# Two-stage kernel on one core: all attention row chunks scaled by VectorE, a new hand-written order with a new bank plan, pooled SBUF rings, and unordered half-row writes

## The chip, the cores and the metric

The kernel runs on one core of one Trainium2 chip. Time is device time in microseconds (us) for one execution; the figures of a kernel are the median of its runs. A profile is one execution taken by the hardware profiler. In this text PE is TensorE (PEld its weight loads), DVE is VectorE, ACT is ScalarE, POOL is GpSimd and SP is the queue that issues most DMAs.

## What is computed

Two blocks follow each other. The first is an attention between a sequence and a small state, both ways, for 8 batches, 8 heads, 512 positions, 32 state rows and 64 columns:

```python
scores = scale * x @ state.T            # softmax over the 32 state rows
xread = softmax(scores) @ state         # 512 rows per head
scores2 = scale * state @ x.T           # softmax over the 512 positions
sread = softmax(scores2) @ x            # 32 rows per head
attn = concatenate([xread, sread])      # (8, 8, 544, 64)
```

The heads are then laid side by side, giving 544 rows of 512 per batch. The second block scores each row with a gate vector and sends the 128 best rows of each batch through two dense layers; all rows are written, the chosen ones changed:

```python
scores = einsum('bsd,d->bs', x, w_gate)
top = argpartition(-scores[b], 128)[:128]
ye = maximum(x[b, top] @ w1, 0) @ w2    # 512 -> 1024 -> 512
out[b, top] = x[b, top] + sigmoid(scores[b, top])[:, None] * ye
```

All arithmetic that decides the result is 32 bit.

## The kernel before

The program is a list of named pieces (function `add`), each with an engine, a function that issues its instructions, the pieces it comes after, and the buffers it takes or uses. Nothing is scheduled automatically: the string `ORDER` lists every piece by hand, and `carry_out` issues them in that order, so each engine works through its own pieces strictly in the listed order. A number behind `@` in the list names the PSUM bank that the piece takes (the tile `banks` has 8 of them, 512 float32 each per partition; `scores` takes two in a row, `read` four). An entry `~n@k` is n transposes of the identity into bank k, whose result nobody reads. Waits between engines follow from the data, and from memory: a tile or a bank that is taken again waits for its last readers.

For each batch b the pieces are:

- `ldx`: loads of x (1 MB in two or four cuts), `ldy`: a second load of x in another layout for batches 6 and 7.
- `turn`/`turned`: transposes of x on PE (L408) and their copies out of PSUM on ACT (L417); batches 6 and 7 use block transposes on DVE instead (`blocks`, L397).
- `stturn`/`stkept`: the transposed state for two batches at a time.
- `scores`: both score matrices at once (L433), in two banks. From them DVE takes the column maximum and subtracts it (`xmax`, `xspread`, `xsub`), ACT takes the exponential (`xexp`); for batches 0 and 1 this is done in halves. `smax` (DVE, L480), `sexp` (ACT, L484) and `ssum` do the same for the other softmax.
- `read`: the attention rows with their sum and gate score as two extra columns (L546; for odd batches, listed in `READ64`, L523, which reads 64 rows at a time from a tile `st_2` that POOL fills with the pieces `beside`). There are two halves r = 0, 1 per batch, each in banks 0 to 3. `zsum` (L562, L563) forms the reciprocal sums, `gate` (L569 to L574) the gate scores, and `rows b.c` scales chunk c of 128 positions and 512 columns into `xs`. Chunks 0 and 2 are scaled by DVE (L556; for odd batches two instructions at L534), chunks 1 and 3 by ACT in eight activations of 64 columns (L554, L532): `ACT_ROWS` lists these.
- `turna`/`turneda`, or for batches 4 to 7 `ablocks`/`aout`/`ain` by DVE and a round trip through DRAM: the transposed weights of the other softmax; `sread` (L627) and `srows` produce the state rows. `stx` and `sts` store both.
- `sgate`, `heads`, `sscore`, `row`/`rowk`/`srowk` or `rowblk`/`rowout`/`rowin`, `win`, `over`, `off`, `oh`, `pick`, `index`, `picked`: the choice of the 128 rows by comparing all scores with each other. `fetch` gathers the rows from DRAM with an indirect DMA on POOL (L659); `parts` on POOL splits the scores for it.
- `xg`/`xgk`: the transposes of the chosen rows (L818, L821); `first b.f`: eight pieces of the first layer (L840); `relu` (L843); `second`: the second layer (L862) in four pieces of two steps each; `add` (L865) adds the gated result to the rows; `put` writes them back with an indirect DMA. The last batch does the second layer in two column halves with two `put`s, so that the first can go early.

Buffers: x has five tiles, the transposed x nine. The exponentials (`eT`, 2), the other softmax (`a`, 2), its block transpose (`a_b`, 1) and its transpose (`aT`, 2) have rings of their own, all with the same number of bytes per tile. The transposed state of all batches has one fixed tile, `st_T`.

## Time and profile before

| what | value |
|---|---|
| median of 3 runs | 212.33 us (211.43 to 213.33) |
| the profiled execution, time of the run | 210.6 us |
| the profiled execution, span from its first to its last instruction | 208.8 us |
| mean granted clock of TensorE in it | 0.961 |

The page gives busy time by engine, the span in 40 slices, DMA queues, the chain of work that ended last, and the costliest groups of instructions (line, engine, operation, tiles, shapes, count, then busy us and mean ns of one, then the engine's idle time ahead of them and what ended it). Other views of the same trace are busy time in chosen windows, the timeline with the idle time before each instruction and its releaser, and the chain in order of time. The lines on which the argument rests stand in the prediction.

### The profile page before, as it was taken

What the parts mean: (1) busy time and instruction counts of PE and PEld (TensorE: products, weight loads), DVE (VectorE), ACT (ScalarE), POOL (GpSimd) and SP (SyncE); (2) the same over time, 40 slices, a digit from 0 to 9 for tenths busy, and PEclk for the clock granted to TensorE, in tenths of its full rate; (3) what the DMA queues carried; (4) which work ended last, traced back from release to release, by engine and by line L of the source; (5) the groups of instructions that cost most, each with busy time, mean ns of one, the idle gap of its engine ahead of it and who ended that gap; (6) DMA issues with size and microseconds to landing.
All of it is one profiled execution on the core that took longest, in us unless ns stands there. A gap on an engine that the chain in (4) does not pass through costs nothing.

```text
span 208.8 us, 5427 instructions
## 1 busy us (share of the span) xinstructions
PE 191.8 (92%) x2196; PEld 146.6 (70%) x2196; DVE 117.4 (56%) x345; ACT 90.3 (43%) x265; POOL 40.2 (19%) x117
## 2 busy tenths in 40 slices
PE   7995895978999999999999999699999999999990
PEld 7664784657997479549756984379749947948980
DVE  3497743898853897328845899995506543001000
ACT  2688676798944334324334446534513211110200
POOL 8600241012021020221021202110212223302022
PEclk9999575799999999999999999999999999999997
DMA  6999999640679364149962954886244430301000
GB/s 202 319 344 387 402 380 324 204 187 17 131 218 262 129 158 96 50 179 186 212 107 53 294 165 121 224 202 232 63 111 156 165 107 0 100 0 53 1 24 26
DMA packets 52628, 34.39 MB, mean 165 GB/s; under 512 B 39164, under 2 KB 47356, under 8 KB 51580
## 3 DMA queue, kind: packets, MB, share of 16 engines
q1 hardware_dynamic: 50508, 29.46, 48.7%
q0 software_dynamic: 1296, 4.20, 6.0%
q10 hardware_dynamic: 800, 0.39, 0.6%
q8 instruction: 17, 0.28, 0.5%
q14 instruction: 7, 0.06, 0.1%
...
## 4 chain that ended last, share of the span: by engine, by line
PE 69%; DVE 11%; ACT 9%; issue 7%; DMA 1%; POOLq 1%; POOL 0%; DVEq 0%; ACTq 0%
PE banks L840 21%; PE banks L862 21%; PE banks L546 5%; PE banks L627 5%; PE banks L523 4%; PE banks L433 3%; PE banks L408 3%; ACT xs L554 3%; ACT a L484 2%; ACT xT L417 2%; PE banks L183 2%; PE banks L818 2%; PE banks L743 1%; DVE a_b L588 1%; DVE mx L456 1%
## 5 line engine op out<-in xcount | busy, mean ns | idle before, releaser
L840 PE MATMUL banks<-xg,w 128*128 128x128 f32 x512 | 61.4, 278 | 0.0
L840 PEld LDWEIGHTS banks<-xg,w 128*128 128x128 f32 x512 | 58.6, 192 | 1.2 <-issue 0.5
L862 PE MATMUL banks<-w,hT 128*128 128x512 f32 (+1 forms) x144 | 59.1, 553 | 0.0
L862 PEld LDWEIGHTS banks<-w,hT 128*128 128x128 f32 x144 | 25.9, 191 | 19.5 <-issue 18.5
L865 DVE SCALAR_TENSOR_TENSOR ot<-banks,z,xr 128x512 f32<-128x512 f32 (+1 forms) x9 | 6.2, 685 | 32.8 <-PE banks L862 32.8
L843 ACT ACTIVATE hT<-banks 128x512 f32<-128x512 f32 x16 | 9.6, 600 | 27.6 <-PE banks L840 27.2
L719 DVE SCALAR_TENSOR_TENSOR win<-srow,sc,after 128x544 bf16<-128x544 f32 (+4 forms) x40 | 18.4, 510 | 3.7 <-DMA srow<-s_d 2.1
L554 ACT ACTIVATE xs<-banks,rz 128x64 f32<-128x64 f32 x64 | 14.0, 330 | 10.9 <-DVE gt L572 10.0
L532 ACT ACTIVATE xs<-banks,rz 128x64 f32<-128x64 f32 x64 | 14.0, 333 | 10.5 <-DVE rz L563 8.8
L659 POOL DMA_INDIRECT out_dram<-ot,idx x7 | 7.9, 1127 | 43.7 <-DVE ot L865 30.0
L484 ACT ACTIVATE a<-banks,nm 128x512 f32<-128x512 f32 x16 | 11.1, 693 | 11.4 <-DVE mx L456 7.8
L659 POOL DMA_INDIRECT xr<-out_dram,idx x8 | 8.3, 1032 | 39.7 <-DVE z L773 21.9
L417 ACT COPY xT<-banks 128x512 f32<-128x512 f32 x23 | 13.3, 598 | 3.6 <-PE banks L408 3.2
L408 PE MATMUL banks<-ident,xf 128*128 128x128 f32 x96 | 13.8, 286 | 1.1 <-ACT xT L417 0.7
L546 PEld LDWEIGHTS banks<-st_v,eT 32*128 32x128 f32 x256 | 9.0, 203 | 6.7 <-issue 5.4
L408 PEld LDWEIGHTS banks<-ident,xf 128*128 128x128 f32 x96 | 10.6, 144 | 4.3 <-ACT xT L417 1.1
L546 PE MATMUL banks<-st_v,eT 32*128 32x66 f32 x256 | 10.3, 295 | 3.3 <-DVE eT L471 3.2
L475 ACT ACTIVATE eT<-eT 128x1024 f32<-128x1024 f32 (+1 forms) x10 | 9.0, 905 | 7.2 <-DVE eT L471 7.2
L480 DVE TENSOR_REDUCE nm<-banks 128x2 f32<-128x1024 f32 x8 | 9.7, 1219 | 3.6 <-PE banks L433 3.6
L471 DVE TENSOR_TENSOR eT<-banks,eT 128x1024 f32<-128x1024 f32 (+1 forms) x10 | 10.1, 1008 | 1.3 <-ACT a L484 1.0
L523 PEld LDWEIGHTS banks<-st,eT 64*128 64x128 f32 x128 | 9.0, 204 | 2.5 <-issue 1.7
L821 ACT COPY xg<-banks 128x512 f32<-128x512 f32 x8 | 4.7, 585 | 13.8 <-PE banks L818 13.7
...
## 6 DMA issues: line engine op xcount, KB each, us to landing
...
```

The source lines that it names most:

```text
L408: nc.tensor.transpose(v[:, k, r], view_x(b)[:, 2 * pair + k, 2 * r:2 * r + 2].rearrange("p w d -> p (w d)"), ident)
L417: nc.scalar.copy(out=t.ap, in_=v)
L484: nc.scalar.activation(out=a.ap[:, g], in_=view_s()[:, :, g], func=AF.Exp, bias=tmp["nm"][:, g:g + 1], accum_out=tmp["ss"][:, g:g + 1])
L523: nc.tensor.matmul(view(o)[:, w, u, 2 * g:2 * g + 2].rearrange("p j m -> p (j m)"), eT.ap[k, w, g, r], st_2[k, READ64.index(b), g], start= ...
L532: nc.scalar.activation(out=to[:, u, j // 2, j % 2], in_=view(o)[:, w, u, j, 0:D], func=AF.Copy, scale=rz[:, u, j:j + 1])
L546: nc.tensor.matmul(view(o)[:, w, q, g], eT.ap[k, w, g, r], st_v[k, b, g], start=True, stop=True)
L554: nc.scalar.activation(out=to[:, q, g], in_=view(o)[:, w, q, g, 0:D], func=AF.Copy, scale=rz[:, q, g:g + 1])
L627: nc.tensor.matmul(o2.ap[k, D * g:D * (g + 1)], aT.ap[:, g, c, k], view_x(b)[:, 4 * g + q, c], start=(c == 0), stop=(c == NC - 1))
L659: touches(b, nc.gpsimd.indirect_dma_start(**kw), True)
L719: nc.vector.scalar_tensor_tensor(wins[c][0:n, 0:SP - f], srow.ap[0:n, f:SP], sc[0:n, b, c:c + 1], after[0:n, 0:SP - f], op0=ALU.is_gt, op1 ...
L840: nc.tensor.matmul(o, w(j), i[:, :, j] if n == 256 else i[:, 0, j], start=(j == 0), stop=(j == ND - 1))
L862: nc.tensor.matmul(py.ap[0:m, 0:part.stop - part.start], hT.ap[:, f, lo:lo + m], w2[:, f, part], start=(f == 0), stop=(f == NF - 1))
```

## The change

Six things change; the arithmetic of the result stays.

1. `READ64` is empty: the odd batches use the same `read` as the even ones (L546), and `st_2`, its memset and the `beside` pieces are gone.
2. `ACT_ROWS` is empty: all four chunks of every batch are scaled by DVE, one instruction of 128x512 each.
3. `ORDER` is a new list with new banks. It holds the same pieces but `beside`. The filling transposes are 40 in eight places (11, 6, 2, 3, 2, 3, 6, 7) instead of 24 in three (14, 5, 5), and they write other columns of their bank. Ahead of the first expert layer, batch 0 goes through its softmax and its first read before the scores of batch 1 are formed. The second halves of rows and the DVE and ACT passes over one score bank follow each other in another order.
4. `eT`, `a`, `a_b` and `aT` share one ring of seven tiles, `R_MID`, and take a tile from it in the order of issue. The transposed state has a ring of four tiles for two batches each. The pool `small` has 4 buffers per name instead of 6.
5. Two `put`s of one batch are declared independent of each other.
6. Code for another way of computing the layers is added (`weight_sums`, `seven`). It runs for the batches in `SEVEN`, which is empty, so nothing of it is issued.

```diff
-    READ64 = (1,3,5,7)
+    READ64 = ()
     ROW_DMA = (3,4,5,6,7)
-    ACT_ROWS = tuple((b, c) for b in range(B) for c in (1, 3))
+    ACT_ROWS = ()
+    SEVEN = ()
+    SUMS_ON_POOL = ()
+    X_BUFS, XT_BUFS, MID_BUFS, XR_BUFS, ST_BUFS = 5, 9, 7, 6, 4
...
-    small = pool("small", 6)
+    small = pool("small", 4)
...
-                    nc.tensor.transpose(banks[:, at[0], 0:128], ident, ident)
+                    nc.tensor.transpose(banks[:, at[0], 384:512], ident, ident)
...
-    R_ET = Ring("eT", [128, 2, 2, 2, 128], 2)
-    R_A = Ring("a", [128, 2, 2, 256], 2)
-    R_AB = Ring("a_b", [128, 2, NC, 4, 32], 1)
-    R_AT = Ring("aT", [128, 2, NC, 128], 2)
+    R_MID = Ring("mid", [128, 2 * NC * 128], MID_BUFS)
...
-    st_T = const.tile([128, B, 2, 128], F32, name="st_T")
+    R_ST = Ring("st_T", [128, 2, 2, 128], ST_BUFS)
...
-    def by_number(b, **kw):
-        touches(b, nc.gpsimd.indirect_dma_start(**kw), True)
+    parts_put = {}
+
+    def by_number(b, columns=None, **kw):
+        st = nc.gpsimd.indirect_dma_start(**kw)
+        touches(b, st, True)
+        if columns is not None:
+            for s in parts_put.setdefault(b, []):
+                tc.declare_no_dep(st.ins, s.ins, reason="other columns of the rows")
+            parts_put[b].append(st)
         nc.gpsimd.memset(z1, 0.0)
```

The order up to the first expert layer, before:

```
ldst0 tables ldx0.0 ldx0.1 ldx0.2 ldx0.3 ldwg exp0 ldx1.0 ldx1.1 ~14@0 stturn0@7 ldx2.0 turn0.0@6 stkept0 ldx2.1 numbers ldst1
turn0.1@5 turned0.0 turn0.2@7 turned0.2 turn0.3@6 turned0.1 turned0.3 stgate0 ~5@0 scores0.0@4 scores0.1 ldw1.0 beside1
turn1.0@7 smax0 turn1.1@6 ldw1.1 turned1.0 turn1.2@3 turned1.1 turn1.3@7 xmax0.0 turned1.2 ldx3.0 scores1.0@0 xmax0.1 turned1.3
turn2.0@6 sexp0.0 xspread0.0 scores1.1 xsub0.0 sexp0.1 ldx3.1 turn2.1@7 ldw2.0 xspread0.1 turn2.2@3 turned2.0 ldw2.1 turn2.3@2
xsub0.1 turned2.2 turna0.0@6 xexp0.0 smax1 stturn2@5 turneda0.0 stturn4@4 ldx4.0 turned2.3 turna0.1@6 xmax1.0 xexp0.1 stturn6@3
xspread1.0 sexp1.0 xsub1.0 sexp1.1 ~5@2 turna1.0@2 xmax1.1 ldx4.1 stkept6 xspread1.1 xsub1.1 turneda1.0 turned2.1 stgate2
read0.0@0 turneda0.1 ssum1 beside3 stkept4 zsum0.0 turna1.1@7 sread0@6 rows0.0 turneda1.1 gate0.0 rows0.1 sread1@7 stgate4
ldx5.0 ldx5.1 row0.0@4 ssum0 beside5 ldx6.0 srows1 read0.1@0 srows0 sgate1 xexp1.0 sgate0 beside7 heads1 stkept2 zsum0.1 heads0
sscore0 sscore1 sts0 rows0.3 rows0.2 turn3.0@5 gate0.1 parts0 row0.1 rowk0 read1.0@0 sts1 srowk0 turned3.0 win0.0 turn3.1@6
...
```

and after:

```
ldst0 tables ldx0.0 ldx0.1 ldx0.2 ldx0.3 ldwg exp0 ldx1.0 ldx1.1 ~11@0 stturn0@7 ldx2.0 ldx2.1 turn0.0@6 stkept0 numbers ldst1
turn0.1@5 turned0.0 turn0.2@4 turned0.2 turn0.3@7 turned0.1 turned0.3 stgate0 ~6@0 scores0.0@4 scores0.1 ldw1.0 turn1.0@7
xmax0.0 turn1.1@6 ldw1.1 turned1.0 turn1.2@3 xspread0.0 turned1.1 turn1.3@7 xsub0.0 turned1.2 ldx3.0 ~2@0 turn2.0@6 turned1.3
smax0 turn2.1@3 xexp0.0 turned2.0 xmax0.1 ldx4.0 ~3@0 turn2.2@7 turned2.1 ldx3.1 turn2.3@6 xspread0.1 turned2.2 ldw2.0
read0.0@0 xsub0.1 turned2.3 stgate2 sexp0.0 stturn2@7 xexp0.1 zsum0.0 stturn4@6 ldw2.1 gate0.0 sexp0.1 rows0.0 stkept2
turna0.0@5 rows0.1 stturn6@4 ssum0 stkept4 read0.1@0 stgate4 ldx4.1 stkept6 scores1.0@6 zsum0.1 scores1.1 rows0.2 turneda0.0
row0.0@4 gate0.1 turna0.1@5 xmax1.0 row0.1 turneda0.1 xmax1.1 rowk0 sread0@5 xspread1.0 xsub1.0 turn3.0@4 ldx5.0 srows0
xspread1.1 xexp1.0 sts0 turned3.0 xsub1.1 turn3.1@4 rows0.3 xexp1.1 ldx5.1 turned3.1 smax1 read1.0@0 stx0 sgate0 turn3.2@4
sexp1.0 zsum1.0 heads0 gate1.0 turned3.2 sscore0 sexp1.1 rows1.0 turn3.3@4 parts0 srowk0 rows1.1 row1.0@7 turned3.3 turna1.0@6
win0.0 read1.1@0 turneda1.0 win0.1 turna1.1@6 win0.2 turn4.0@5 turneda1.1 zsum1.1 turned4.0 rows1.2 ~2@4 sread1@6 rows1.3
scores2.0@4 gate1.1 ldx6.0 scores2.1 ssum1 stx1 win0.3 srows1 sts1 turn4.1@3 win0.4 turn4.2@2 smax2 turned4.1 over0@1 turned4.2
turn4.3@3 ldx6.1 off0 sexp2.0 row1.1 oh0 turn5.0@2 turned4.3 turna2.0@0 sgate1 xmax2 turned5.0 heads1 pick0 turneda2.0 ~3@3
scores3.0@2 rowk1 scores3.1 xspread2 sexp2.1 turn5.1@7 turn5.2@0 srowk1 smax3 turned5.1 turned5.2 turna2.1@7 xsub2 sexp3.0
turn5.3@0 turneda2.1 index0 turna3.0@5 xexp2 picked0 fetch0 xmax3 sread2@7 turneda3.0 xspread3 sexp3.1 below0 ldy6.0 turned5.3
~6@4 turna3.1@5 xsub3 exps0 turneda3.1 ~7@4 sread3@5 win1.0 xexp3 win1.1 read2.0@0 ldx7.0 ssum3 ldx7.1 win1.2 srows3 xg0@4
zsum2.0 ldy6.1 xgk0 sgate3 rows2.0 heads3 first0.0@4 sts3 rows2.1 first0.1 sscore3 win1.3 first0.2 win1.4 sscore1 ldy6.2
...
```

Behind the first layer both lists weave the pieces of batches 2 to 7 between the layers of the batches before them, in differing order; in the new list `blocks7` come with the second layer of batch 2 (before: one there, three with that of batch 3), and `over1` follows `first0.2` (before: ahead of `first0.0`).

More of the change, by code (lines that the diff above doesn't have):

```diff
@@ L24 @@
-    xsub0.1 turned2.2 turna0.0@6 xexp0.0 smax1 stturn2@5 turneda0.0 stturn4@4 ldx4.0 turned2.3 turna0.1@6 xmax1.0 xexp0.1 stturn6@3
-    xspread1.0 sexp1.0 xsub1.0 sexp1.1 ~5@2 turna1.0@2 xmax1.1 ldx4.1 stkept6 xspread1.1 xsub1.1 turneda1.0 turned2.1 stgate2
-    read0.0@0 turneda0.1 ssum1 beside3 stkept4 zsum0.0 turna1.1@7 sread0@6 rows0.0 turneda1.1 gate0.0 rows0.1 sread1@7 stgate4
-    ldx5.0 ldx5.1 row0.0@4 ssum0 beside5 ldx6.0 srows1 read0.1@0 srows0 sgate1 xexp1.0 sgate0 beside7 heads1 stkept2 zsum0.1 heads0
@@ L28 @@
-    sscore0 sscore1 sts0 rows0.3 rows0.2 turn3.0@5 gate0.1 parts0 row0.1 rowk0 read1.0@0 sts1 srowk0 turned3.0 win0.0 turn3.1@6
-    xexp1.1 stx0 zsum1.0 scores2.0@4 turned3.1 ldx6.1 rows1.0 scores2.1 gate1.0 rows1.1 turn3.2@6 win0.1 win0.2 turned3.2 smax2
-    read1.1@0 win0.3 turn3.3@6 sexp2.0 zsum1.1 turned3.3 gate1.1 rows1.2 rows1.3 parts1 turn4.0@6 win0.4 xmax2 turned4.0 stx1
-    turna2.0@3 sexp2.1 xspread2 turn4.1@6 row1.0@2 turned4.1 row1.1 scores3.0@0 xsub2 rowk1 scores3.1 srowk1 turneda2.0 over0@7
@@ L32 @@
-    smax3 turn4.2@6 xexp2 turn4.3@5 turn5.0@4 turned4.3 off0 oh0 turn5.1@3 sexp3.0 turn5.2@5 xmax3 turn5.3@2 turned5.1 pick0
-    sexp3.1 turna3.0@3 picked0 index0 fetch0 xspread3 turna2.1@7 turneda3.0 turneda2.1 turna3.1@3 xsub3 turned5.0 sread2@7 below0
-    turneda3.1 turned5.3 sread3@4 win1.0 ldy6.0 xexp3 win1.1 read2.0@0 ldx7.0 turned4.2 win1.2 ldx7.1 exps0 turned5.2 ssum3 xg0@6
-    win1.3 srows3 win1.4 xgk0 sts3 sgate3 over1@5 ssum2 heads3 first0.0@6 off1 srows2 oh1 sts2 first0.1 sscore3 zsum2.0 rows2.0
@@ new lines @@
+    zsum2.0 ldy6.1 xgk0 sgate3 rows2.0 heads3 first0.0@4 sts3 rows2.1 first0.1 sscore3 win1.3 first0.2 win1.4 sscore1 ldy6.2
+    gate2.0 parts1 over1@6 ssum2 read2.1@0 sigmoid0 srows2 sts2 off1 oh1 row2.0@5 sgate2 pick1 first0.3 zsum2.1 ldy6.3 gate2.1
+    heads2 picked1 row2.1 index1 below1 relu0.0 rows2.2 first0.4@6 fetch1 exps1 rowk2 rows2.3 first0.5 srowk2 sigmoid1 stx2 win2.0
+    first0.6 sscore2 scores4.0@4 win2.1 parts2 scores4.1 win2.2 first0.7 win2.3 smax4 second0.0.0@7 relu0.4 xmax4 second0.0.2
@@ L432, in scores @@
                     half = slice(D * w, D * (w + 1))
-                    nc.tensor.matmul(view_s()[Ns * q:Ns * (q + 1), w, g], st_T[half, b, g, Ns * q:Ns * (q + 1)],
+                    nc.tensor.matmul(view_s()[Ns * q:Ns * (q + 1), w, g], st_T[b][0].ap[half, st_T[b][1], g, Ns * q:Ns * (q + 1)],
                                      xT[2 * g + q // 2].ap[half, q % 2].rearrange("p r t -> p (r t)"), start=True, stop=True)
@@ L882, in layers, with halves_of, weight_sums @@
                 add(f"put{G}.{k}", "POOL", put, after=p_a[-1:] + p_n, uses=[ot, u["idx"]])
+    def halves_of(w):
+        n, m = w.shape[1] // 2, w.shape[2] // 2
+        return w[:, 0:n, 0:m], w[:, 0:n, m:2 * m], w[:, n:2 * n, 0:m], w[:, n:2 * n, m:2 * m]
+    p_sums = {}
+    def weight_sums(used):
+        for k, (w, t, p_w) in enumerate(((w1, t1, p_w1), (w2, t2_, p_w2))):
+            b11, b12, b21, b22 = halves_of(w)
+            steps = [(t[:, 0], b12, b11), (t[:, 1], b22, t[:, 0]), (b12, b22, b12), (t[:, 2], b21, t[:, 1])]
+            p = []
+            for n, (o, i, j) in enumerate(steps):
+                p.append(add(f"wsum{k}.{n}", "POOL", lambda o=o, i=i, j=j: nc.gpsimd.tensor_tensor(out=o, in0=i, in1=j, op=ALU.subtract),
+                             after=list(p_w) + ([p[0]] if n in (1, 2) else [p[1]] if n else []) + (used if n == 2 else [])))
+            p_sums[k] = {"p1": p_w[0], "p2": p_w[-1], "p3": p_w[-1], "p5": p[0], "p6": p[1], "p7": p[2], "p4": p[3]}
@@ L899 @@
         if chosen and ((n_tiles == 1 and any(b == g[-1] for g in GROUPS)) or b == B - 1):
-            layers(chosen, b == B - 1)
+            if len(chosen) == 2 and chosen[0]["b"] in SEVEN:
+                if not p_sums:
+                    weight_sums([p for p in pieces if p.name.startswith(("first", "second"))])
+                seven(chosen, b == B - 1)
+            else:
+                assert not p_sums
+                layers(chosen, b == B - 1)
             chosen = []
```

225 lines of the change are left out of this document (172 added, 53 removed).

## The prediction

> **What bounds the kernel now.** I read the page first, then busy time by window, then the timeline of TensorE with the releaser of each wait, then the group rows for durations.
>
> ```profile
> span 208.8 us, 5427 instructions
> PE 191.8 (92%) x2196; PEld 146.6 (70%) x2196; DVE 117.4 (56%) x345; ACT 90.3 (43%) x265; POOL 40.2 (19%) x117
> PEclk9999575799999999999999999999999999999997
> ```
>
> TensorE is busy 92% of the span, but its granted clock falls to a half between 20 and 40 us. The next view cuts the span at the start of the first expert layer (56.78) and at TensorE's end (203.90); the columns are stretch, length, busy us of PE, PEld, DVE, ACT, POOL, then clock and DMA.
>
> ```profile
> 9.20:56.78 47.58, 39.36 (x670) 31.28 (x663) 35.40 (x91) 37.28 (x100) 7.20 (x25) 0.86 0.79 268
> 56.78:110.00 53.22, 52.89 (x535) 39.06 (x538) 32.72 (x98) 20.70 (x67) 8.03 (x21) 1.00 0.65 158
> 110.00:140.00 30.00, 28.30 (x375) 20.02 (x372) 25.99 (x67) 14.51 (x49) 4.17 (x13) 1.00 0.64 178
> 140.00:203.90 63.90, 63.80 (x566) 50.02 (x564) 19.56 (x80) 13.42 (x43) 12.69 (x29) 1.00 0.28 85
> 203.90:208.80 4.90, 0.00 (x0) 0.00 (x0) 0.48 (x1) 0.00 (x0) 1.07 (x2) 0.73 0.07 27
> ```
>
> So there are two regimes. From 56.78 to 203.90, 147.1 us, TensorE idles only 0.33 + 1.70 + 0.10 = 2.1 us: that part is TensorE's work and an order can't shorten it by more. Before 56.78 TensorE is idle 47.58 - 39.36 = 8.2 us of this window and at half clock for part of the rest, while ScalarE (37.28) and VectorE (35.40) share the load. Whoever brings the first expert layer forward brings the end forward by as much. The timeline says what TensorE waits for there (brackets: idle time before, releaser), and the chain of waits shows how one such wait is built:
>
> ```profile
> 21.80 1.99 PE L546 MATMUL banks<-st_v,eT 32*128 32x66 f32 x32 [3.19 <-DVE eT L471]
> 33.91 0.69 PE L706 MATMUL banks<-ident,sc 128*128 128x128 f32 x2 [2.23 <-DVE sc L574]
> 56.78 2.92 PE L840 MATMUL banks<-xg,w 128*128 128x128 f32 x24
> 31.10 1.75 ACT xs L554 x8
> 32.88 0.69 DVE xs L556
> ```
>
> The chunk scaled by ScalarE (eight activations, 1.75 us) stands in the chain ahead of VectorE's own chunk (0.69): the two share the four banks of a half-read and take turns. 56.78 is where the first expert layer of batch 0 starts.
>
> **The rows, costed.** The groups with shapes apart give the durations (busy us, mean ns of one):
>
> ```profile
> L532 ACT ACTIVATE xs<-banks,rz 128x64 f32<-128x64 f32 x64 | 14.0, 333 | 10.5 <-DVE rz L563 8.8 <-DVE gt L569 1.8
> L554 ACT ACTIVATE xs<-banks,rz 128x64 f32<-128x64 f32 x64 | 14.0, 330 | 10.9 <-DVE gt L572 10.0 <-DVE xs L556 0.8
> L534 DVE TENSOR_TENSOR xs<-banks,rz 128x256 f32<-128x256 f32 x16 | 6.0, 417 | 0.2
> L556 DVE TENSOR_TENSOR xs<-banks,rz 128x512 f32<-128x512 f32 x8 | 5.5, 690 | 4.6 <-ACT xs L554 4.5
> L562 DVE TENSOR_SCALAR rz<-banks 128x16 f32<-128x16 f32 x16 | 2.7, 166 | 7.9 <-PE banks L546 4.8 <-PE banks L523 3.0
> L563 DVE RECIPROCAL rz<-rz 128x16 f32<-128x16 f32 x16 | 4.0, 253 | 0.6
> L719 DVE SCALAR_TENSOR_TENSOR win<-srow,sc,after 128x544 bf16<-128x544 f32 (+4 forms) x40 | 18.4, 510 | 3.7 <-DMA srow<-s_d 2.1
> 86.06 1.10 PE banks L523 x16
> 138.01 1.05 PE banks L546 x32
> ```
>
> ScalarE loses 16 chunks, 28.0 us; VectorE gains 16 x 0.69 = 11.0 us, less the odd batches' pairs that become one instruction: 8 x (6.0/8 - 0.69) = 0.5. On TensorE an odd batch's half-read goes from 16 records in 1.10 us to 32 in 1.05: 8 x -0.05 = -0.4, six of the eight behind the first layer (-0.3). The four `beside` copies and the memset of their tile leave POOL, which nobody waits for once the copies are gone: nothing on the path.
>
> **The new order ahead of the first layer.** TensorE's pieces ahead of `first0.0` are the same in both orders but for `over1`, which moves behind it, and the filling transposes. What carries the stretch is VectorE's queue. Its difference: the four scalings `rows0.1`, `rows0.3`, `rows1.1`, `rows1.3` come in (+2.76), `zsum2.0` comes in (0.17 + 0.25 = +0.42), batch 1's two remaining pairs shrink (-0.1); `win1.3`, `win1.4`, `ssum2`, `sscore1` move behind (0.5, 0.3 and 0.25 by estimates from L719's row, whose means run with the width, and from the small L562 row: -1.1). So 35.40 becomes about 37.4 us of work. Starting at 9.2, VectorE can let `first0.0` go at 9.2 + 37.4 = 46.6 if it never idles, and at 58.8 if it idles as now (47.58 - 35.40 = 12.2). ScalarE, 37.28 - 4 x 1.75 = 30.3, no longer competes.
>
> Between these ends I walked the new order by hand, each engine in its own order, a bank being free when its last reader is done, 0.2 us allowed from a last matmul to its reader. More rows for that:
>
> ```profile
> L408 PE MATMUL banks<-ident,xf 128*128 128x128 f32 x96 | 13.8, 286 | 1.1 <-ACT xT L417 0.7 <-ACT st_T L383 0.4
> L417 ACT COPY xT<-banks 128x512 f32<-128x512 f32 x23 | 13.3, 598 | 3.6 <-PE banks L408 3.2
> L480 DVE TENSOR_REDUCE nm<-banks 128x2 f32<-128x1024 f32 x8 | 9.7, 1219 | 3.6 <-PE banks L433 3.6
> L471 DVE TENSOR_TENSOR eT<-banks,eT 128x512 f32<-128x512 f32 x4 | 2.8, 692 | 1.0 <-ACT a L484 1.0
> 13.05 1.53 PE L408 MATMUL banks<-ident,xf 128*128 128x128 f32 x12
> 45.49 1.02 PE banks L433 x32
> ```
>
> Up to batch 2's turns (now 13.05 to 14.2, bound by the loads of x) little changes; only `scores1` (1.02) is put off. Batch 0's column passes run on VectorE without a stop (seven of 0.7 or 1.22 us) from 9.2 to 14.6, where ScalarE's `sexp` passes used to alternate on the same banks. `read0.0` follows at 14.0 in place of 21.8. Then ScalarE is late: `sexp0.1` ends at 17.4 and frees bank 5 for `turna0.0` (TensorE idles 1.3), and `stkept4` frees bank 6 for `scores1.0` at 19.7. `read0.1` 18.3, `sread0` to 23.9, `turn3.1` waits for its bank at 24.4 (1.55, the longest gap), `read1.0` 26.4, `read1.1` 30.2 behind `rows1.1`, `sread1` to 33.6, `scores2` to 34.6, `pick0` 38.4, `scores3` to 39.8, `sread2` to 44.6, `sread3` to 48.3, `read2.0` to 49.4, `sgate3` 50.4, `heads3`, and `first0.0` at 50.7. VectorE idles some 4 us in that walk. The fetch of batch 0's rows is issued near 43.3, 6 us ahead of its transposes, so it isn't late. I take the walk: 50.7 - 56.78 = -6.1 us, ends -10.2 (46.6) and +2.0 (58.8).
>
> **The clock.** The granted clock in this case moves in steps 3.41 us apart:
>
> ```profile
> 18.44:21.85 3.41, 0.21 (x6) 0.08 (x4) 2.50 (x5) 3.16 (x7) 0.00 (x0) 1.00 1.07 385
> 21.85:28.68 6.83, 6.83 (x166) 6.15 (x166) 3.69 (x13) 3.75 (x13) 2.81 (x10) 0.50 1.06 395
> 28.68:32.09 3.41, 2.92 (x42) 2.21 (x40) 1.40 (x10) 3.27 (x12) 0.71 (x3) 1.00 1.09 383
> 32.09:38.92 6.83, 5.01 (x47) 3.49 (x54) 3.84 (x14) 3.57 (x13) 0.79 (x4) 0.50 0.93 311
> 42.33:45.74 3.41, 2.42 (x32) 1.89 (x40) 3.27 (x7) 3.29 (x13) 0.60 (x3) 1.00 0.33 139
> 1.34 3.25 PE banks L183 x14
> 7.73 0.55 PE banks L183 x5
> ```
>
> A step with 0.21 us busy is followed by two at 0.50, and so is one with 2.92 busy of small-row reads; one with 2.42 of full transposes is not. A halved stretch of 6.83 us costs at most half its busy time, 3.4 us. The walk has no gap over 1.6 us, and 16 more fillers stand in its gaps (16 x 0.11 = 1.8 us of idle time, which cost nothing while another engine is awaited); but its steps from 18 to 29 us hold many small-row reads too. Ends 0 and +5.9 (both stretches back, half of 6.83 + 5.01); I take +0.5, near none, since VectorE carries that stretch. The Trainium skill's page "TensorE: Matmul & The Clock Gate", Part 4, says that transposes don't count as busy for this gate; here 14 transposes alone at 232 ns each were followed by five at 110, so the trace speaks against it. By the page the fillers would be no help and both halved stretches would come back: some 3 us more than my sum.
>
> **Behind the first layer.** `over1` comes in (0.35 to 0.46; I take 0.4), the half-reads give -0.3. Of the 2.1 us idle now, the largest is this one:
>
> ```profile
> 135.66 0.63 PE L818 MATMUL banks<-ident,xr 128*128 128x128 f32 x4 [1.58 <-DVE a_b L588]
> 80.99 0.35 PE banks L743 x15
> 201.73 2.38 DMA out_dram<-ot,half
> 203.91 0.48 DVE L865 SCALAR_TENSOR_TENSOR ot<-banks,z,xr 128x256 f32<-128x256 f32 x1 [2.98 <-PE banks L862]
> 204.90 0.96 POOL L659 DMA_INDIRECT out_dram<-ot,half  x1 [2.09 <-DVE ot L865]
> ```
>
> VectorE's 78.3 us there (32.72 + 25.99 + 19.56) become about 86, still 59% of the stretch. The new order moves `blocks7` ahead of the crowd at 110 to 140 but fills the first 40 us (layers of batches 0 and 1) almost to the brim. I take idle time as now, 2.1 (ends 0.3, the walk's, and 2.1 + 3 should the early stretch stall as often as 110 to 140 did, twice 1.58). Sum: +0.1, ends -2 and +3.
>
> **Other edits.** The independent puts: the first half's write lands at 201.73 + 2.38 = 204.11, the second half's values are ready at 203.91 + 0.48 = 204.39, so the wait removed is over already; next late is VectorE. Between -0.3 and +0.3, taken as 0. The shared ring of seven tiles, four state tiles and `small` at 4: every tile is taken again about two batches later, when its reader has run in the walk; 0, hidden by the walk's order, and if a reader were late the taker's engine would wait for it.
>
> **Sum.** -6.1 + 0.5 + 0.1 + 0 = -5.5: span 203.3, and the profiled run, 210.6 for a span of 208.8, becomes 205.1. That run lies 1.7 under the median of 212.33; on the median, 206.8.
>
> **The rivals.**
> (1) VectorE's idle time doesn't shrink. For it: it waits for ScalarE and TensorE in turn now, 12.2 us of it. Against: four ScalarE chunks that it took turns with are gone. `first0.0` at 58.8, +2.0, and crowded early layers of +0.5: 214.8. It decides once VectorE idles over 56.78 - 9.2 - 37.4 = 10.2 us ahead of the first layer.
> (2) The clock halves twice again, for want of dense steps between 18 and 29 us. Half of the 5.9 us falls on the path: 206.8 - 0.5 + 3 = 209.3 (this is also the page's case).
> (3) VectorE hardly idles: rows read as durations overlap by some hundredths at each end, so my walk is long. `first0.0` at 47.5: 203.6.
>
> **How the numbers follow.** Forecast 0.60 (its own range 205 to 209), rival 1 0.13, rival 2 0.14, rival 3 0.13. From 202.5 to 212.5 all but most of rival 1 and a tail of rival 3 are held. About 1%, 2.1 us, is what a measurement of this kernel can tell from no change. Faster by more than that (under 210.2): the forecast, rival 3 and part of rival 2, less the forecast's slow tail, 0.77; slower (over 214.5): most of rival 1, 0.11; the rest, 0.12.
>
> **What would show it.** Right: the first matmul of the first expert layer near 50.7; no releaser on TensorE over 2 us; the clock at 1.00 from 5 us on, or one halved stretch; ScalarE near 62 us busy, VectorE near 127; the last 4.9 us unchanged. Wrong: a first layer no earlier than 55, TensorE idle over 4 us behind it, or two halved stretches.

## The result, and the profile after

| | before | after |
|---|---|---|
| median | 211.88 us (210.88 to 213.33, 4 runs) | 201.94 us (201.74 to 202.85, 4 runs) |
| profiled execution, run / span | 210.6 / 208.8 us | 201.74 / 200.0 us |
| first matmul of the first expert layer | 56.78 us | 49.82 us |
| from there to TensorE's end | 147.12 us | 145.28 us |
| from TensorE's end to the end of the span | 4.90 us | 4.90 us |

The change made the kernel faster: ratio of the times 0.953, 95% interval 0.947 to 0.960. The direction was forecast, but the time lies 0.6 us below the forecast range of 202.5 to 212.5. In the tables, medians hold all runs of a kernel, and ratios leave out those over 1.5% above its fastest.

The first lines of the page after: span, busy time by engine, granted clock in 40 slices, and the group that now scales all rows.

```profile
span 200.0 us, 5582 instructions
PE 187.9 (94%) x2340; PEld 145.5 (73%) x2340; DVE 124.2 (62%) x353; ACT 63.0 (32%) x137; POOL 35.6 (18%) x100
PEclk9999999999999999999999999999999999999998
L564 DVE TENSOR_TENSOR xs<-banks,rz 128x512 f32<-128x512 f32 x32 | 21.1, 682 | 0.3
```

ScalarE gives up 27.3 us of busy time (90.3 to 63.0) and VectorE takes on only 6.8 (117.4 to 124.2). The clock, which fell to a half in two stretches before, is whole from end to end.

Busy time by window, cut at the new start of the first expert layer and at TensorE's end (stretch, length, then busy us of PE, PEld, DVE, ACT, POOL, granted clock, DMA share, GB/s):

```profile
9.20:49.82 40.62, 35.95 (x729) 28.82 (x714) 36.76 (x87) 31.09 (x68) 2.40 (x7) 1.00 0.97 319
49.82:195.10 145.28, 144.56 (x1574) 109.97 (x1574) 83.78 (x257) 27.62 (x62) 26.61 (x67) 1.00 0.49 131
195.10:200.00 4.90, 0.04 (x1) 0.00 (x0) 0.48 (x1) 0.00 (x0) 1.08 (x2) 0.89 0.08 27
```

Of the 8.80 us by which the span is shorter, 6.96 lie ahead of the first layer (47.58 to 40.62) and 1.84 behind it; the last 4.90 are as before. Ahead of the layer TensorE's idle time fell from 8.22 us to 40.62 - 35.95 = 4.67, and its busy time from 39.36 to 35.95, although the stretch holds 18 fillers more than before (23 for 5): all of its work runs at full clock. Behind it, TensorE idles 145.28 - 144.56 = 0.72 us where it idled 2.13.

The waits of TensorE, summed by line and releaser (us in total, times, longest; the first three and the last):

```profile
PE banks L416 <- ACT xT L425: 1.6, 2, 1.0
PE banks L189 <- POOL ident masks.py:199: 1.3, 1, 1.3
PE banks L620 <- ACT mid L492: 1.1, 1, 1.1
...
PE banks L554 <- DVE xs L564: 0.2, 1, 0.2
```

The two longest waits of before are gone: 3.19 us for VectorE's `eT` ahead of the first read, and 2.23 for `sc`. What is left ahead of the layer is ScalarE's copies and softmax passes, 1.1 us at a time, as the walk of the prediction had it. For the rows themselves (L554, a read waiting for banks that are still being scaled) TensorE waits 0.2 us in all.

The places of the walk on TensorE's timeline (start, length, what, and in brackets the idle time before it and its releaser):

```profile
14.55 1.12 PE L554 MATMUL banks<-st_v,mid 32*128 32x66 f32 x32
...
17.74 0.66 PE L620 MATMUL banks<-ident,mid 128*128 128x128 f32 x4 [1.07 <-ACT mid L492]
...
18.76 1.12 PE L554 MATMUL banks<-st_v,mid 32*128 32x66 f32 x32
20.02 1.10 PE L441 MATMUL banks<-xT,st_T 64*32 64x256 f32 x32
...
25.91 0.66 PE L416 MATMUL banks<-ident,xf 128*128 128x128 f32 x4 [1.05 <-ACT xT L425]
26.50 1.12 PE L554 MATMUL banks<-st_v,mid 32*128 32x66 f32 x32
...
47.44 1.12 PE L554 MATMUL banks<-st_v,mid 32*128 32x66 f32 x32
```

The walk had `read0.0` at 14.0, `turna0.0` at 17.4 behind 1.3 us of idle time, `read0.1` at 18.3, `scores1` at 19.7, `turn3.1` behind a gap of 1.55, `read1.0` at 26.4. All of them are there, within 0.6 us. The walk is late at its end only: the last line, `read2.0`, ends at 48.56 where the walk had 49.4.

What the walk took for granted is less clear: "what carries the stretch is VectorE's queue". The chain of work that ended last, followed back from the first expert layer to 9.2 us and added up by engine, says otherwise:

| chain from 9.2 us to the first layer, us | TensorE | ScalarE | VectorE | other |
|---|---|---|---|---|
| before | 26.0 | 13.6 | 6.3 | 1.6 |
| after | 23.1 | 9.5 | 6.7 | 1.2 |

VectorE is busy for 36.76 of the 40.62 us, so it leaves little room, but what the stretch lost came off ScalarE (4.1) and TensorE (2.9).

### The profile page after: what moved, and what is told of

It is laid out like the page before. It is cut to its first block, busy times and chain, and to the rows that moved or that the text cites. A ratio compares the mean times of both kernels' runs of the same rounds, so it can differ in the third digit from the quotient of the medians.

```text
span 200.0 us, 5582 instructions
## 1 busy us (share of the span) xinstructions
PE 187.9 (94%) x2340; PEld 145.5 (73%) x2340; DVE 124.2 (62%) x353; ACT 63.0 (32%) x137; POOL 35.6 (18%) x100
## 4 chain that ended last, share of the span: by engine, by line
PE 78%; issue 6%; DVE 5%; ACT 5%; DMA 3%; POOL 1%; POOLq 1%; ACTq 0%; DVEq 0%
PE banks L856 26%; PE banks L878 24%; PE banks L554 7%; PE banks L416 4%; PE banks L635 4%; PE banks L441 3%; PE banks L834 2%; DMA st_v<-in_state_dram 2%; PE banks L620 2%; PE banks L189 1%; PE banks L758 1%; DVE mid L479 1%; DVE xs L564 1%; DMA mid<-a_d 1%; ACT xT L425 1%
## 5 line engine op out<-in xcount | busy, mean ns | idle before, releaser
L856 PE MATMUL banks<-xg,w 128*128 128x128 f32 x512 | 62.7, 279 | 0.0
L878 PE MATMUL banks<-w,hT 128*128 128x512 f32 (+1 forms) x144 | 57.9, 547 | 0.0
L564 DVE TENSOR_TENSOR xs<-banks,rz 128x512 f32<-128x512 f32 x32 | 21.1, 682 | 0.3
L554 PE MATMUL banks<-st_v,mid 32*128 32x66 f32 x512 | 17.9, 276 | 0.2 <-DVE xs L564 0.2
L554 PEld LDWEIGHTS banks<-st_v,mid 32*128 32x128 f32 x512 | 15.7, 186 | 2.7 <-issue 1.0
L492 ACT ACTIVATE mid<-banks,nm 128x512 f32<-128x512 f32 x16 | 11.1, 694 | 11.8 <-DVE nm L488 9.0
L483 ACT ACTIVATE mid<-mid 128x1024 f32<-128x1024 f32 (+1 forms) x10 | 8.9, 894 | 8.7 <-DVE mid L479 4.5
L635 PE MATMUL banks<-xf,mid 128*32 128x64 f32 x512 | 9.4, 221 | 0.9 <-ACT mid L623 0.5
L479 DVE TENSOR_TENSOR mid<-banks,mid 128x1024 f32<-128x1024 f32 (+1 forms) x10 | 10.0, 996 | 0.2
L635 PEld LDWEIGHTS banks<-xf,mid 128*32 128x32 f32 x512 | 7.8, 110 | 3.0 <-issue 1.6
```

The costliest lines, as they stand in the source:

```text
L479: nc.vector.tensor_tensor(out=e, in0=s.ap if r is None else view_e(s.ap, r), in1=e, op=ALU.subtract)
L492: nc.scalar.activation(out=a.ap[:, g], in_=view_s()[:, :, g], func=AF.Exp, bias=tmp["nm"][:, g:g + 1], accum_out=tmp["ss"][:, g:g + 1])
L554: nc.tensor.matmul(view(o)[:, w, q, g], eT.ap[k, w, g, r], st_v[k, b, g], start=True, stop=True)
L564: nc.vector.tensor_tensor(out=to, in0=view(o)[:, w, :, :, 0:D], in1=rz.unsqueeze(3).to_broadcast([128, 4, 2, D]), op=ALU.mult)
L635: nc.tensor.matmul(o2.ap[k, D * g:D * (g + 1)], aT.ap[:, g, c, k], view_x(b)[:, 4 * g + q, c], start=(c == 0), stop=(c == NC - 1))
L856: nc.tensor.matmul(o, w(j), i[:, :, j] if n == 256 else i[:, 0, j], start=(j == 0), stop=(j == ND - 1))
```

## The experiments

The prediction put the gain down to one thing, a shorter stretch ahead of the first layer, and credited the order and the rows' move together. That left open which of the parts carries it. The theories to be told apart: the rows alone; the order alone; the two only together; the clock, held up by the fillers; and, for the remainder, the smaller edits. Line numbers are those of the new kernel, unless said otherwise; where an edit shortens the list of pieces they shift.

All results in one table ("first layer" and "behind" are read from the profiled execution; ratios are against the kernel before, run on the same chip beside it):

| kernel | order | scaled by ScalarE | median us | ratio (95%) | first layer | behind |
|---|---|---|---|---|---|---|
| after, first measurement | new | none | 201.94 | 0.953 (0.947 to 0.960) | 49.82 | 145.28 |
| after, again | new | none | 201.85 | 0.956 (0.954 to 0.959) | 50.18 | |
| e1 | new | chunks 1, 3 of all | 209.74 to 215.13 | | 55.73 | 147.27 |
| e2 | old | none | 209.88 | 0.994 (0.990 to 0.998) | 56.66 | 146.24 |
| e8 | old, no `READ64` | none | 213.67 | 1.006 (1.001 to 1.010) | 59.30 | |
| e4 | old, more fillers | chunks 1, 3 of all | 212.95 | 1.011 (1.002 to 1.020) | 58.73 | 146.07 |
| e9 | new | 1, 3 of batches 0, 1 | 206.2 | 0.976 (0.972 to 0.980) | 55.87 | 143.83 |
| e14 | new | 3 of batches 0, 1 | 205.9 | 0.971 (0.965 to 0.978) | 54.12 | |
| e15 | new | 1 of batches 0, 1 | 205.0 | 0.973 (0.969 to 0.976) | 54.39 | |
| e10 | new | 1, 3 of batches 2 to 7 | 205.04 | 0.972 (0.967 to 0.978) | 50.32 | 147.28 |
| e3 | new, 17 of 40 fillers | none | 200.32 | 0.949 (0.942 to 0.956) | 49.20 | |
| e11 | new, no fillers | none | 200.17 | 0.949 (0.944 to 0.953) | 49.29 | 143.81 |
| e13 | e11 again | none | 200.99 | 0.953 (0.951 to 0.956) | 48.84 | 145.26 |
| e5 | new, puts in order | none | 201.03 | 0.953 (0.949 to 0.957) | 49.60 | |
| e6 | new, with `READ64` | none | 201.16 | 0.950 (0.944 to 0.956) | 49.09 | |
| e7 | new, old rings | none | 202.44 | 0.956 (0.950 to 0.962) | 49.56 | |

### The order without the rows, and the rows without the order

The new list and its bank plan were put in together in every run, so "order" below means both. In the new kernel, ScalarE gets its chunks back:

```diff
-    ACT_ROWS = ()
+    ACT_ROWS = tuple((b, c) for b in range(B) for c in (1, 3))
```

> The new kernel with one edit undone: chunks 1 and 3 are scaled by ScalarE again (eight activations of 1.75 us together in place of one VectorE instruction of 0.68), in the new order. Theory A (the rows carry the gain: ScalarE's chunk holds the banks of each half-read and stands in line with VectorE's): the four chunks ahead of the first expert layer cost at least 1.1 us each, the first layer starts at 54 or later and the time is 206 to 209. Theory B (the order carries the gain, and ScalarE has time to spare now): first layer within 1.5 us of 49.8, time 201 to 203.5. Theory C (the clock carries the gain) has no part in this run unless the clock halves: then 204 or more with a halved stretch in the record.

In the kernel before, VectorE gets all rows:

```diff
-    ACT_ROWS = tuple((b, c) for b in range(B) for c in (1, 3))
+    ACT_ROWS = ()
```

> The kernel before with one edit done alone: all chunks scaled by VectorE, old order, old banks, the 64-row reads kept. Theory A: 4 x (1.75 - 0.7) = 4.2 us and the turns saved ahead of the first layer, so 206 to 209. Theory B: the old order puts other waits in the place of these, and VectorE, at 26.0 of 30 us between 110 and 140, gets 3 us more there: 211 to 215. Theory C: no change but for the clock, 210 to 213, with the two halved stretches still there.

The first gave 209.74, 210.85, 215.03 and 215.13 us, with mean clocks of 0.971, 0.966, 0.940 and 0.940; they lie too far apart for a ratio, but none is more than 1% under the 211.28 of the kernel before beside it. The second gave 209.88, a gain of 0.2 to 1.0%. Its windows (ahead of and behind its first layer), its clock, and its longest waits:

```profile
9.20:56.66 47.46, 37.91 (x663) 30.64 (x661) 37.86 (x98) 31.18 (x70) 7.20 (x25) 0.89 0.79 269
56.66:202.90 146.24, 144.57 (x1465) 108.79 (x1464) 84.71 (x262) 27.58 (x61) 24.89 (x63) 1.00 0.49 131
```

```profile
PE banks L546 <- DVE eT L471: 3.2, 1, 3.2
PE banks L408 <- ACT xT L417: 2.1, 1, 2.1
```

So in the old order 27 us less on ScalarE leave the first layer where it was (56.66): the wait of the first read for `eT` stands as before, since the old list forms the scores of batch 1 and passes them on before batch 0's read, and has them in banks 0 and 1, which the read takes (`scores1.0@0`, `read0.0@0`); and the clock still falls. The chain from 9.2 us to the first layer now lies on VectorE for 19.5 us, where it lay for 6.3 before: in the old order VectorE's passes come in the place of ScalarE's.

In the new order, ScalarE's chunks undo nearly all the gain. The windows of that kernel:

```profile
9.20:55.73 46.53, 41.07 (x708) 33.07 (x698) 34.54 (x83) 37.53 (x100) 2.39 (x7) 0.89 0.86 281
55.73:203.00 147.27, 144.70 (x1574) 110.40 (x1574) 77.16 (x245) 47.84 (x158) 26.53 (x67) 1.00 0.48 129
```

Its first layer is at 55.73, and TensorE idles 147.27 - 144.70 = 2.57 us behind it. Apart the two edits give about 0 and 1.4 us (211.28 to 209.88), together 9.9: they work only together. Neither "the rows alone" nor "the order alone" holds.

A third kernel took both row edits, `ACT_ROWS` and `READ64`, into the old order:

```diff
-    READ64 = (1,3,5,7)
+    READ64 = ()
-    ACT_ROWS = tuple((b, c) for b in range(B) for c in (1, 3))
+    ACT_ROWS = ()
     # and the four beside pieces leave ORDER
```

> The kernel before with both row edits (all chunks scaled by VectorE, the 64-row reads and their copies gone) in the old order. The first edit alone gave 209.9 against 211.3 there. If the order is what turns the edits into time, 208.5 to 210.5 and a first layer no earlier than 55.5. If the edits carry the gain once both are made, 204 to 207.

213.67, no gain (ratio 1.006). Its ten runs go with their clock, from 211.47 us at 0.966 to 215.63 at 0.940. Its first layer in the table, 59.30, is that of an execution of 215.4 us, the second longest of the ten, and isn't to be set beside the others.

### The clock alone

The kernel before with more fillers in its two long gaps, and the new columns for them:

```diff
-    ... ~5@2 turna1.0@2 ...
+    ... ~26@2 turna1.0@2 ...
-    ... parts0 row0.1 rowk0 ...
+    ... parts0 ~18@4 row0.1 rowk0 ...
-    nc.tensor.transpose(banks[:, at[0], 0:128], ident, ident)
+    nc.tensor.transpose(banks[:, at[0], 384:512], ident, ident)
```

> The kernel before with more filling transposes in front of its two long waits of TensorE: 26 in place of 5 ahead of the second transposes of batch 1, and 18 more between the first transposes of batch 3 and the second score row; they write the last quarter of their bank. Theory C: the clock stays whole, the two halved stretches go and the time falls by 3 to 6 us: 206 to 209. Theories A and B: VectorE and ScalarE carry that stretch, a whole clock is worth at most 2 us: 210 to 213.

212.95, a ratio above 1. One halved stretch is left of two, as the slices of its page show, and a wait for VectorE of 2.5 us stands in the list of its waits:

```profile
PEclk9999985999999999999999999999999999999997
```

```profile
PE banks L662 <- DVE scr L626: 2.5, 1, 2.5
```

The first layer starts at 58.73, later than before. So these fillers neither kept the clock whole nor brought the layer forward. They don't price a whole clock: one halved stretch stayed, and 39 more transposes at 0.11 us are some 4.3 us of work on TensorE by estimate from the prediction's row.

The other way round, the new kernel without its fillers, all or those behind the first two groups:

```diff
-    ... ldx1.1 ~11@0 stturn0@7 ... stgate0 ~6@0 scores0.0@4 ... ~2@0 ... ~3@0 ... ~2@4 ... ~3@3 ... ~6@4 ... ~7@4 ...
+    ... ldx1.1 stturn0@7 ... stgate0 scores0.0@4 ...
```

> The new kernel without the 23 filling transposes behind the sixth place in the order (2, 3, 2, 3, 6 and 7 of them), the first 11 and 6 kept; no result changes. Theory C: without them the granted clock falls to a half in at least one stretch of 6.8 us ahead of the first layer and the time is 203.5 to 206. Theories A and B: fillers stand in waits, so nothing is won or lost: 201 to 203, clock 0.99 or more. If the fillers were in the way of work, 199 to 201.

> The new kernel without any filling transposes, the first 11 and 6 too. Without the late ones alone it took 200.3. If the first ones are needed to bring the clock up, the first turns and scores run at half speed, which delays the first exponentials by 1 to 2 us: 201 to 203. If they only fill a wait for the loads and for ScalarE, 199.5 to 200.7.

> The new kernel without filling transposes once more, beside the new kernel on the same chip. If the 40 fillers stand in the way of work, 1 to 2 us less than the base. If they only fill waits and the difference before (200.2 against 201.9) was one between chips, within 0.6 us of the base.

200.32, 200.17 and 200.99. The mean clock of their twelve runs is 0.993 to 1.000: it stays up without a single filler. The page of the first no-filler kernel:

```profile
PE 181.3 (92%) x2300; PEld 139.5 (70%) x2300; DVE 124.3 (63%) x353; ACT 63.3 (32%) x137; POOL 35.4 (18%) x100
PEclk9999999999999999999999999999999999999999
```

TensorE has 6.6 us less to do and nothing comes later. The fillers are therefore not what keeps the clock up in the new order. They may cost a little: beside the new kernel on the same chip, taking them all out went from 201.85 to 200.99, ratios 0.956 (0.954 to 0.959) and 0.953 (0.951 to 0.956). The intervals overlap, so that 0.9 us isn't settled. The version without fillers is the fastest that was run, if by little.

### Which of ScalarE's chunks cost what

The chunks of the first two batches are scaled ahead of the first layer, those of the other six mostly behind it. Two kernels split them:

```diff
-    ACT_ROWS = ()
+    ACT_ROWS = tuple((b, c) for b in (0, 1) for c in (1, 3))        # e9
+    ACT_ROWS = tuple((b, c) for b in range(2, B) for c in (1, 3))   # e10
```

> The new kernel with ScalarE scaling chunks 1 and 3 of batches 0 and 1 only, the ones ahead of the first expert layer. If what the ScalarE rows cost lies in the early stretch (5.9 of the 7.9 us of the span in the run with all of them), 206 to 210, first layer at 54 or later. If the clock takes a part in it, the record shows halved stretches there and the runs differ by their clock; if it is only the banks, the clock is at 0.99 or more and the time is 205 to 206.5. If the cost lies behind the first layer, 201 to 203.

> The new kernel with ScalarE scaling chunks 1 and 3 of batches 2 to 7 only, all behind the first expert layer. First layer at 49.5 to 50.5, clock 0.99 or more. TensorE was idle 2.6 us behind the first layer with all chunks on ScalarE and 0.7 with none, so 203 to 204.5; if that idle came from the late start alone, 201.5 to 202.5.

206.2 and 205.04. Beside them on the same chip ran the new kernel with its puts in order, 201.03 (below: the puts are worth nothing), so four chunks early cost 5.2 us and twelve late ones 4.0. The sum, 201.03 + 9.2 = 210.2, is within what the kernel with all sixteen gave.

The early ones first. The timeline of e9 about the second half-read of batch 0, all engines, with some rows left out:

```profile
16.95 0.68 DVE L564 TENSOR_TENSOR xs<-banks,rz 128x512 f32<-128x512 f32 x1
...
17.79 0.59 ACT L391 ACTIVATE st_T<-banks 64x512 f32<-64x512 f32 x1
...
18.39 1.75 ACT L562 ACTIVATE xs<-banks,rz 128x64 f32<-128x64 f32 x8
...
19.58 1.72 PE L554 MATMUL banks<-st_v,mid 32*128 32x66 f32 x32 [1.13 <-ACT xs L562]
...
21.24 1.10 PE L441 MATMUL banks<-xT,st_T 64*32 64x256 f32 x32
21.41 0.18 DVE L570 TENSOR_SCALAR rz<-banks 128x16 f32<-128x16 f32 x1 [2.19 <-PE banks L554]
```

VectorE has scaled its chunk by 17.63. ScalarE can't start on the other until 18.39, for it is still copying the transposed state, and then holds the banks to 20.14. `read0.1`, which writes the same four banks, waits 1.13 us, begins 0.56 us ahead of the end of ScalarE's activations, and takes 1.72 us, 0.60 more than in the new kernel. `scores1` follows at 21.24 in place of 20.02, and VectorE stands idle for 2.19. The new order puts the next half-read close behind a scaling, so that it meets what holds the banks at once. The Trainium skill's page "PSUM — Partial Sum Buffer", in its section on bank collisions, has two engines' accesses to one bank kept apart by waits, reads too; the traces agree, in the wait just shown and in one of ScalarE for VectorE's chunk (0.35 us, below). In the new kernel the same two chunks are one stretch of VectorE, as its row in the timeline shows:

```profile
17.24 1.28 DVE L564 TENSOR_TENSOR xs<-banks,rz 128x512 f32<-128x512 f32 x2
```

The chain that ended last leaves the same chunk by another way, ScalarE's own queue: behind the chunk stand copies of the state and then `turneda0.0` (L623), for which TensorE's later work waits. It comes 1.2 us later than in the new kernel (e9 first, then the new kernel):

```profile
22.43 0.59 ACT L623 COPY mid<-banks 128x512 f32<-128x512 f32 x1
```

```profile
21.21 0.59 ACT L623 COPY mid<-banks 128x512 f32<-128x512 f32 x1
```

The second price is the clock. e9's trace has it halved for 10.25 us, and those of two smaller variants (below) for 6.83 us each. In e9's trace this is the larger price. Its `read1.0` and `scores2`, and `scores2` in the new kernel (whose `read1.0` is at 26.50, above):

```profile
28.18 1.87 PE L554 MATMUL banks<-st_v,mid 32*128 32x66 f32 x32 [0.38 <-ACT xs L562]
...
40.12 1.09 PE L441 MATMUL banks<-xT,st_T 64*32 64x256 f32 x32
```

```profile
33.83 1.09 PE L441 MATMUL banks<-xT,st_T 64*32 64x256 f32 x32
```

Up to `read1.0` e9 has lost 1.7 us, from there to `scores2`, where the halved stretch lies and the chain stays almost wholly on TensorE, 4.6 more (11.94 for 7.33), and behind it nothing. The two smaller variants:

```diff
-    ACT_ROWS = ()
+    ACT_ROWS = ((0, 3), (1, 3))   # e14
+    ACT_ROWS = ((0, 1), (1, 1))   # e15
```

> The new kernel with ScalarE scaling chunk 3 of batches 0 and 1 only (two chunks of the four that cost 4 us together). If each chunk costs the hold of its banks, about 1 us each and a whole clock: 203 to 204 with the clock at 0.99. If most of the 4 us is a clock that halves once the waits pass some length, either 201.5 to 202.7 with a whole clock or 205 to 206 with a halved one.

> The new kernel with ScalarE scaling chunk 1 of batches 0 and 1 only. Chunk 1 stands ahead of the second half-read in the same banks, chunk 3 does not, so the hold of the banks should cost more here than for chunk 3: 203 to 204.5 with a whole clock. If the clock is the cost, a halved stretch stands in the record and 205 to 206; without one, within 1 us of the base.

205.9 and 205.0, against 201.85 for the new kernel on the same chip (its expectation, and its result in the table):

> The new kernel unchanged, as the base of this set. 201 to 202.5 against 211 to 212, ratio 0.947 to 0.958, first layer at 49.1 to 50.5.

The slices of e9, e14 and e15:

```profile
PEclk9999985699999999999999999999999999999999
```

```profile
PEclk9999985999999999999999999999999999999999
```

```profile
PEclk9999589999999999999999999999999999999999
```

Two chunks on ScalarE are enough for a halved stretch. The four runs of e14 tell the two prices apart: 203.10 us at a mean clock of 0.995, like the new kernel's own (0.993 to 0.999), and 205.7, 206.11 and 207.18 at 0.982, 0.982 and 0.973. The first has ScalarE's chunks without the clock: 203.10 - 201.85 = 1.25 us, 0.6 for each chunk, from a single run. One halved stretch of 6.83 us (the profiled run is that of 206.11) adds 2.6 to 3.0 (205.7 and 206.11 less 203.10). This price comes from runs of one kernel that differed in their clock, not from an experiment that sets the clock alone. Whether chunk 1 costs more than chunk 3, as e15's expectation had it, stays open: its four runs lie at clocks of 0.983 to 0.992, none as high as the new kernel's, and the least of them is 204.69.

The late chunks cost in another way. e10's runs are 203.94 and 204.33 us at clocks of 0.996 and 0.999, and 205.76 and 205.86 at 0.989, so with a whole clock some 3 of the 4.0 us remain. In the profiled execution, 204.33, the clock is whole and the layer starts at 50.32, but the stretch behind it is 2.0 us longer than in the new kernel:

```profile
50.32:197.60 147.28, 144.70 (x1574) 110.37 (x1574) 77.16 (x245) 47.94 (x158) 26.52 (x67) 1.00 0.48 129
```

TensorE idles 2.58 us in it, in place of 0.72. Against the profile of e5, which ran beside it, the stretch is 3.3 us longer (143.95 there, 0.17 of it idle). Its longest wait is this one. The timeline of e10 there, all engines:

```profile
124.10 0.69 DVE L564 TENSOR_TENSOR xs<-banks,rz 128x512 f32<-128x512 f32 x1
...
124.87 1.75 ACT L562 ACTIVATE xs<-banks,rz 128x64 f32<-128x64 f32 x8 [0.35 <-DVE xs L564]
126.46 0.57 ACT L640 ACTIVATE xt<-banks,rs 128x64 f32<-128x64 f32 x2
...
127.07 0.29 DVE L685 SCALAR_TENSOR_TENSOR scr<-xt,wg_s 128x128 f32<-128x128 f32 x1 [2.28 <-ACT xt L640]
...
127.42 0.41 PE L689 MATMUL banks<-same_n,part_s 128*128 128x32 f32 x2 [1.95 <-DVE scr L685]
```

and the same place in the new kernel, VectorE's row and TensorE's:

```profile
123.55 1.29 DVE L564 TENSOR_TENSOR xs<-banks,rz 128x512 f32<-128x512 f32 x2
124.75 0.28 DVE L685 SCALAR_TENSOR_TENSOR scr<-xt,wg_s 128x128 f32<-128x128 f32 x1
```

```profile
125.10 0.41 PE L689 MATMUL banks<-same_n,part_s 128*128 128x32 f32 x2 [0.25 <-DVE scr L685]
```

The state rows `xt` (L640) are ScalarE's, and are listed behind its chunk of rows. ScalarE waits for VectorE's chunk, works 1.75 us, then does `xt`; VectorE waits 2.28 us for that, and TensorE 1.95 for VectorE. With the chunk on VectorE, TensorE waits 0.25. That one wait is 1.7 us of the 1.9 more that TensorE idles against the new kernel's profile. The cost isn't ScalarE's load (it is busy a third of the time there) but its place in a chain that goes from engine to engine.

### The smaller edits

In the new kernel, the declared independence of the puts replaced by nothing; `READ64` and the `beside` pieces brought back; and rings of their own (2, 2, 1, 2 tiles) in place of the shared one:

```diff
-                tc.declare_no_dep(st.ins, s.ins, reason="other columns of the rows")
+                pass
...
-    READ64 = ()
+    READ64 = (1,3,5,7)
...
-    R_MID = Ring("mid", [128, 2 * NC * 128], MID_BUFS)
+    R_MID = Ring("mid", [128, 2 * NC * 128], 2)
+    R_A2 = Ring("a2", [128, 2 * NC * 128], 2)
+    R_AB = Ring("a_b", [128, 2 * NC * 128], 1)
+    R_AT = Ring("aT", [128, 2 * NC * 128], 2)
```

> The new kernel with one edit undone: the second half-row write of the last batch waits for the first again. Theory: the first write has landed before the second's values are ready (204.11 against 204.39 in the kernel before), so nothing changes: 201.3 to 202.6. Rival: the wait costs POOL a landing, 1 to 2 us at the very end: 203 to 204.

> The new kernel with one edit undone: the odd batches read 64 rows at a time again from the tile that POOL fills (all rows still scaled by VectorE, in two instructions for the odd batches). By the prediction's price, 8 x 0.05 us on TensorE and 8 x 0.06 us on VectorE: within 1 us of the new kernel, 201 to 203. Rival: the copies on POOL hold up the reads of batch 1 and VectorE's extra instructions delay the first layer: 203 to 205.

> The new kernel with the exponentials, the other softmax and its two transposes in rings of their own again (2, 2, 1 and 2 tiles, seven in all as now). If the shared ring only renames memory, 201 to 203. Rival: with one ring a tile comes free earlier where the new order needs it, and without it the single block-transposed tile holds VectorE up behind the first layer: 203 to 205, with more idle time on TensorE behind the first layer than 0.7 us.

201.03, 201.16 and 202.44, with ratios of 0.953, 0.950 and 0.956, each interval overlapping the new kernel's. For the puts and `READ64` nothing can be told from no change. For the rings a little may remain: e7's runs (201.84 to 202.62) lie above all of e6, which ran beside it with the shared ring (200.87 to 201.54), though e7's idle time behind the first layer is 0.8 us, not more than the new kernel's. The state tiles and `small` were not tried alone. For the puts, the end of the new kernel's timeline shows why:

```profile
191.78 0.48 DVE L881 SCALAR_TENSOR_TENSOR ot<-banks,z,xr 128x256 f32<-128x256 f32 x1 [9.90 <-PE banks L878]
193.05 1.00 POOL L669 DMA_INDIRECT out_dram<-ot,half  x1 [9.73 <-issue]
...
195.24 0.48 DVE L881 SCALAR_TENSOR_TENSOR ot<-banks,z,xr 128x256 f32<-128x256 f32 x1 [2.98 <-PE banks L878]
196.00 0.97 POOL L669 DMA_INDIRECT out_dram<-ot,half  x1 [1.84 <-DVE ot L881]
```

The second `put` waits for VectorE's last values, as it did; the write of the first makes no difference that the last 4.90 us show.

## Why the prediction was right in its way and wrong in its size

The forecast was -5.5 us of span; measured are -8.8. By its own terms:

| term | forecast (ends) | measured |
|---|---|---|
| ahead of the first layer | -6.1 (-10.2, +2.0) | -6.96 |
| clock | +0.5 (0, +5.9) | 0: whole throughout |
| behind the first layer | +0.1 (-2, +3) | -1.84 |
| puts | 0 (-0.3, +0.3) | 0: the last 4.90 us unchanged |
| rings, `small` | 0 | `R_MID`: 1.3 at most (e7 against e6); the others not tried alone |
| from the profiled run to the median | +1.7 | +0.2 |

**Ahead of the first layer: right in time, not in what carries it.** The walk gave 50.7 for 49.82, with some 4 us of idle time on VectorE; there are 40.62 - 36.76 = 3.86. It is long by 0.9. VectorE's work came out 0.6 shorter, 36.76 us instead of 37.4. Two chunks back to back take 1.28 us, not twice 0.69, which is the mechanism of rival 3; but with three such pairs ahead of the layer that is 0.3, and it isn't shown to be what brought the layer forward: the walk meets the end of `sread2` to 0.1 us (44.47 for 44.6) and is late only behind it (`sread3` ends at 47.51 for 48.3), where TensorE waits for nothing longer than 0.22 us. Rival 1 would have left the layer at 58.8. That the chain lies on VectorE for only 6.7 us means that "VectorE carries that stretch" was not the reason for the time; the walk, which follows every engine and every bank, did not rest on it.

**The clock: right in kind.** No halved stretch came, so the 0.5 kept for one was too much, and rival 2 fell. Its reason was wrong on both sides, though: the forecast let the fillers help to hold the clock, and without any fillers it holds as well. In the new order the profiles with ScalarE's rows in the first two batches have it halved (e9, e14, e15); in the old one it falls with VectorE's rows too (e2). The Trainium skill's page "TensorE: Matmul & The Clock Gate", Part 4, says that transposes don't count as busy for the gate; the row of 14 transposes at 232 ns followed by five at 110 speaks against it by the durations alone, for the granted clock in the profile of before reads 1.00 over both. And that the two stretches stayed away is no evidence for either side, since the fillers turned out not to matter.

**Behind the first layer: the step that failed.** The prediction said "I take idle time as now, 2.1", and counted the twelve late chunks as load that VectorE can bear (86 us of 147; measured 83.8 of 145.3). It can. But the idle time of before was not a property of the stretch that an order keeps: with ScalarE's chunks the new order idles 2.6 us there (e1, e10), without them 0.7, and the old order without them 1.7 (e2: 146.24 - 144.57). So both edits take part here too, as ahead of the layer. With the walk's own end for the idle time, 0.3 in place of 2.1, the term would have been -1.7. The rest of the 1.9, some 0.5, is TensorE's work, 144.56 us where +0.1 on 144.99 was expected; executions of the same list differ by more than that (143.66 in e9 and 144.56 here, for the same 1574 records), so nothing is read into it. The whole stretch scatters likewise, at a clock of 1.00: 143.81 and 145.26 us in e11 and e13, which are one kernel, and 143.8 to 145.5 with 0.15 to 0.8 us idle in all the profiles of the new order that have their late chunks on VectorE. The -1.84 is therefore one draw of a term that may come out some 1.5 larger; why was not found.

**The step to the median.** The profiled run of before lay 1.7 under its median, and the forecast carried that over as a constant. It isn't one. Before's runs scatter with the clock: of the 13 beside e1 the fastest, 209.85 us, has a mean clock of 0.975 and the slowest, 212.70, has 0.953. With the halved stretches that scatter goes too: the four runs of after lie at clocks of 0.995 to 1.000, and the profiled one 0.2 under the median. That is 1.5 us of the error of 4.9, as much as any term but the one behind the layer.

**The range** reached down to 202.5 and should have held 201.9. It was drawn about the rivals, the lowest of which was 203.6, and not from the ends of the terms: a stretch behind the layer at its lower end (-2) with the other terms as forecast gives 204.7, and without the clock's 0.5 and the constant 1.7 it gives 202.5, before any shortening of the walk.

**The rest.** ScalarE is busy for 63.0 us (forecast near 62), VectorE for 124.2 (near 127). The -0.3 for `READ64` can't be told from nothing (e6).

What stays open: the clock's price by an experiment of its own, the 0.9 us of the fillers, the scatter behind the first layer, and how the gain divides between the new order and its banks. Moving `scores1` out of banks 0 and 1 in the old order, which is what the 3.19 us wait of before hangs on, was not tried.
